# First weight piece loaded ahead of x, x transposed chunk by chunk as it lands, two M products issued earlier: a fused attention and MLP kernel on one Trainium2 core

## Chip, cores, metric

One core of a Trainium2 chip, everything in float32. The metric is device time in microseconds of one execution, median over runs. "Span" is the time from the first to the last instruction in the profile of one execution; it is about 1.8 us less than the time. Each run also records the mean clock granted to TensorE over its span: "full" is 1.00, "half" is 0.50, and a stretch at half clock is called a spell.

Engines: PE is TensorE's matmuls, PEld its weight loads, DVE VectorE, ACT ScalarE, POOL GpSimd, SP SyncE (here only a DMA queue).

## The reference, cut

```python
B, H, S, Ns, D = 8, 8, 512, 32, 64          # x: (B,H,S,D), state: (B,H,Ns,D)
scores  = x @ state.T / sqrt(D); a  = softmax(scores);  xread = a @ state
scores2 = state @ x.T / sqrt(D); a2 = softmax(scores2); sread = a2 @ x
t = concat([xread, sread], axis=2) as (B*(S+Ns), H*D) = 4352 tokens of 512
h = t @ w_in                                 # 512 x 2048, given as float64
g = h * sigmoid(1.702 * h)
out = g @ w_out                              # 2048 x 512, given as float64
```

The weights arrive as float64 words; DVE and ACT turn each piece of 128 rows and 512 columns into float32 ("rounding").

## The kernel before

The state of a batch is folded into w_in first: M = state x w_in (per chunk of 512 columns), then h = a x M, so that the token side needs two matmul steps per block and not four. Batches 0 and 1 run while the weights still come in; batches 2 to 7 then run on PE almost without holes. The parts that the change touches:

```python
def load_x(b):
    ...
    for c in range(SCH):                     # four chunks of 128 tokens
        queue = nc.scalar if b == 0 and c % 2 else nc.sync
        queue.dma_start(xn[b][:, c], x_v[b, c])

def round_a(i):                              # "power step" of piece i
    nc.vector.tensor_scalar(sc, hi, 0x7FF00000, None, ALU.bitwise_and)           # DVE
    ...                                      # w_in: two ACT instructions (Relu) finish it
def round_b(i):                              # the rest: four DVE instructions
    ...

def att_xT(b, j, warm=0):                    # transpose head pair j, all four chunks
    ps = att_ps([P, SCH, P], f"xT_{b}_{j}")
    for c in range(SCH):
        if warm: keep_warm(warm)             # filler matmuls, result unused
        nc.tensor.transpose(ps[:, c], x_heads(b, c, j), ident)
    (nc.vector.tensor_copy if b == 0 and j % 2 == 0 else nc.scalar.copy)(A[b]["xT"][:, j], ...)

def att_M(b, c, spare=False):                # 16 small matmuls, then two ACT copies
    ...
    for g in range(NG):
        nc.scalar.copy(m[:, g], ps[g])

def turn(b, c, then, n=()):                  # the four h products of batch b, chunk c
    for i in range(nper):
        if i == nper - 1 and then:
            att_M(*then)
        up_x(b, nper * c + i)
        if i < len(n): rounds(n[i])          # n[i] pieces rounded after product i

# ... opening
load_state(0); load_x(0); load_weights(NPR); load_state(1); load_x(1); load_weights(2 * NPR)
keep_warm(8)
att_state(0)
att_xT(0, 0, 2)
for j in range(1, NPR): att_xT(0, j)
att_scores(0)
powers_to(1); att_blocks(0); att_x_exp(0)    # softmax of batch 0 begins
powers_to(2); round_to(2, 1); att_x_norm(0)
keep_warm(24)
... # state, x and scores of batch 1
keep_warm(24)
powers_to(4); round_to(NPR, 2)               # pieces 0 to 3 rounded: chunk 0 complete
att_M(0, 0)
```

PSUM tiles of state, xT, M and eT share one pool of two buffers; h has two of its own. In the profiles, stT and xT are the transposed state and x, s the scores, aT the transposed softmax of the token side, e the exponentials (eT transposed), g the gelu of h, o the first products with w_out, and warm the filler. "later" and "sums" are buffers used for several things in turn.

## Time and profile before

| | before |
|---|---|
| time, median of the 4 runs beside the changed kernel | 803.94 us (802.64 to 805.23) |
| span of the profiled run, mean granted clock | 800.5 us, 0.997 |
| PE busy | 782.1 us (98%), of which part is filler |
| first h product starts | 34.99 us |
| first product with w_out ("o") starts | 88.67 us |

### The profile page before, as it was taken

The numbers are of one execution on the slowest core, as the hardware profiler recorded it, in microseconds if no ns is written. First come the engines' busy times: TensorE is split into PE (matmuls) and PEld (weight loads), VectorE is DVE, ScalarE is ACT, GpSimd is POOL, SyncE is SP. The second block draws the span as 40 slices with busy tenths as digits, with TensorE's granted clock in tenths as the row PEclk, the third lists the DMA queues.
The fourth block names the chain that finished last, engine by engine and source line by source line (L and its number), as shares of the span: only waits on it lengthen the run. The fifth ranks groups of instructions, "written<-read, shape, count | busy, mean of one in ns | idle before, by whom it ended". The sixth has DMA issues, their size and how long they took to land.

```text
span 800.5 us, 8798 instructions
## 1 busy us (share of the span) xinstructions
PE 782.1 (98%) x3618; PEld 530.4 (66%) x3620; DVE 314.4 (39%) x669; ACT 219.4 (27%) x394; POOL 36.1 (5%) x72
## 2 busy tenths in 40 slices
PE   8989999999999999999999999999999999999996
PEld 3333464467865878487856786487847788874785
DVE  3998899443404070226104340407022520312220
ACT  3676511023123141323133222314132312103100
POOL 0000000010100011000100011000100010010011
PEclk9999999999999999999999999999999999999998
DMA  9711345010030004000030003000300000010001
GB/s 238 293 54 52 105 137 133 1 52 1 27 83 0 1 17 91 1 1 14 27 69 1 1 28 83 0 1 14 84 9 1 14 27 14 0 23 5 1 14 39
DMA packets 43624, 35.17 MB, mean 44 GB/s; under 512 B 37312, under 2 KB 37312, under 8 KB 43584
## 3 DMA queue, kind: packets, MB, share of 16 engines
q1 hardware_dynamic: 37920, 25.17, 11.6%
q0 software_dynamic: 3584, 8.92, 3.4%
q10 hardware_dynamic: 2080, 0.52, 0.3%
q8 instruction: 28, 0.46, 0.2%
q14 instruction: 12, 0.10, 0.0%
HBM read 25.69 MB, written 8.91 MB: 43 GB/s over the span
## 4 chain that ended last, share of the span: by engine, by line
issue 69%; PE 22%; POOL 4%; DVE 2%; ACT 1%; DMA 1%; SPq 0%; POOLq 0%
PE h L404 7%; PE o L429 7%; POOL out_dram L491 4%; PE y L472 2%; PE x L472 2%; PE M L267 1%; PE z L472 1%; PE sr L359 1%; DMA xn<-in_x_dram 1%; PE xT L259 0%; ACT M L342 0%; PE s L267 0%; DVE w_in L199 0%; DVE w_in L198 0%; DVE later L197 0%
## 5 line engine op out<-in xcount | busy, mean ns | idle before, releaser
L404 PE MATMUL h<-aT,M 128*128 128x512 f32 x512 | 223.9, 594 | 5.8 <-ACT M L342 5.8
L404 PEld LDWEIGHTS h<-aT,M 128*128 128x128 f32 x512 | 96.5, 190 | 127.5 <-issue 113.6
L406 ACT ACTIVATE g<-h 128x512 f32<-128x512 f32 x120 | 71.5, 597 | 179.9 <-PE h L404 179.9
L472 PE MATMUL x<-w_out,g 128*128 128x256 f32 x448 | 100.0, 379 | 0.0
L472 PEld LDWEIGHTS x<-w_out,g 128*128 128x128 f32 x448 | 84.2, 190 | 13.9 <-issue 3.4
L453 DVE TENSOR_TENSOR later<-g,g 128x256 f32<-128x256 f32 (+1 forms) x64 | 26.1, 408 | 152.7 <-ACT g L406 152.7
L342 ACT COPY M<-M 128x512 f32<-128x512 f32 x64 | 33.2, 595 | 96.9 <-PE M L267 96.9
L491 POOL DMA_DIRECT2D out_dram<-osb x56 | 30.2, 543 | 541.7 <-ACT osb L488 359.7
L472 PE MATMUL z<-sums,later 128*128 128x256 f32 x224 | 51.1, 382 | 0.0
L472 PE MATMUL z<-w_out,g 128*128 128x256 f32 x224 | 50.8, 381 | 0.0
L472 PE MATMUL y<-sums,later 128*128 128x256 f32 x224 | 50.5, 379 | 0.0
L472 PE MATMUL y<-sums,g 128*128 128x256 f32 x224 | 50.5, 379 | 0.0
L472 PE MATMUL y<-w_out,g 128*128 128x256 f32 x224 | 50.1, 382 | 0.0
L472 PEld LDWEIGHTS y<-w_out,g 128*128 128x128 f32 x224 | 42.1, 190 | 10.5 <-issue 5.0
L472 PEld LDWEIGHTS z<-sums,later 128*128 128x128 f32 x224 | 42.1, 190 | 10.5 <-issue 5.0
L490 DVE TENSOR_TENSOR osb<-z,later 128x256 f32<-128x256 f32 x28 | 10.6, 420 | 92.3 <-PE z L472 92.3
L472 PEld LDWEIGHTS y<-sums,g 128*128 128x128 f32 x224 | 42.1, 190 | 5.5
L472 PEld LDWEIGHTS z<-w_out,g 128*128 128x128 f32 x224 | 41.6, 190 | 5.2
L472 PEld LDWEIGHTS y<-sums,later 128*128 128x128 f32 x224 | 41.6, 190 | 5.2
L499 DVE TENSOR_TENSOR later<-y,later 128x512 f32<-128x512 f32 x7 | 4.8, 692 | 87.8 <-PE y L472 87.8
L260 ACT COPY xT<-xT 128x512 f32<-128x512 f32 x30 | 17.6, 587 | 63.4 <-PE xT L259 63.4
L267 PE MATMUL M<-w_in,stT 64*32 64x512 f32 x512 | 33.7, 594 | 0.4 <-DVE w_in L199 0.4
(105 smaller groups left out, 748.6 us busy)
## 6 DMA issues: line engine op xcount, KB each, us to landing
later<-in_moe_w_out_dram SPq DMA_DIRECT2D x16, 512.0 KB
out_dram<-osb POOLq DMA_DIRECT2D x56, 128.0 KB, 2.0
xn<-in_x_dram SPq DMA_DIRECT2D x26, 256.0 KB
w_out<-in_moe_w_in_dram SPq DMA_DIRECT2D x12, 512.0 KB
later<-in_moe_w_in_dram SPq DMA_DIRECT2D x4, 512.0 KB
sums<-in_x_dram SPq DMA_DIRECT2D x4, 256.0 KB
out_dram<-osb POOLq DMA_DIRECT2D x4, 256.0 KB, 2.4
stn<-in_state_dram SPq DMA_DIRECT2D x16, 32.0 KB
```

Source lines behind the costliest of these rows:

```text
L260: (nc.vector.tensor_copy if b == 0 and j % 2 == 0 else nc.scalar.copy)(A[b]["xT"][:, j], ps.rearrange("p c q -> p (c q)"))
L267: nc.tensor.matmul(ps[g][st], A[b]["stT"][rows, st], rhs(rows, j), start=True, stop=True)
L342: nc.scalar.copy(m[:, g], ps[g])
L359: nc.tensor.matmul(ps[:, j], x_heads(b, c, j), a["eT"][:, :, c, Ns * j : Ns * (j + 1)], start=(c == 0), stop=(c == SCH - 1),)
L404: nc.tensor.matmul(hps, lhs[i], rhs[i], start=(i == 0), stop=(i == n - 1))
L406: nc.scalar.activation(out=gt[:, :ntok], in_=hps, func=AF.Gelu_apprx_sigmoid)
L429: nc.tensor.matmul(ops, G[key, f][:, P * r : P * (r + 1)], w_out[:, f], start=(f == 0), stop=(f == NF - 1))
L453: nc.vector.tensor_tensor(out=s1, in0=a21, in1=a22, op=ALU.add)
L472: nc.tensor.matmul(ps[:, r], lhs[f][:, P * r : P * (r + 1)], rhs[:, f], start=(first and r == 0 and f == 0), stop=(f == HF - 1), skip_grou ...
L490: nc.vector.tensor_tensor(out=o[:, r], in0=ps[:, r], in1=with_[:, r], op=ALU.add)
L491: nc.gpsimd.dma_start(dst(nb * i + r, slice(HN * k, HN * (k + 1))), o[:, r])
L499: nc.vector.tensor_tensor(out=k2, in0=Y, in1=k1, op=ALU.add)
```

## The change

Intent: give DVE its first piece of weights while it would otherwise wait for x; transpose x as it lands; and hide the copies of two M products behind an h product.

```diff
-            queue = nc.scalar if b == 0 and c % 2 else nc.sync
-            queue.dma_start(xn[b][:, c], x_v[b, c])
+            nc.sync.dma_start(xn[b][:, c], x_v[b, c])
...
+    def att_xT_arriving(b, warm):
+        A[b]["xT"] = apool.tile([P, NPR, S], FP32, tag="xT", name=f"xT_{b}")
+        for c in range(SCH):
+            keep_warm(warm)
+            ps = att_ps([P, NPR, P], f"xT_{b}_{c}")
+            for j in range(NPR):
+                nc.tensor.transpose(ps[:, j], x_heads(b, c, j), ident)
+            (nc.scalar.copy if c % 2 else nc.vector.tensor_copy)(A[b]["xT"][:, :, P * c : P * (c + 1)], ps)
...
+    load_weights(1)
     load_state(0)
     load_x(0)
...
-    keep_warm(8)
+    keep_warm(11)
+    round_to(1, 0)
     att_state(0)
-    att_xT(0, 0, 2)
-    for j in range(1, NPR):
-        att_xT(0, j)
+    att_xT_arriving(0, 2)
     att_scores(0)
-    powers_to(1)
+    powers_to(2)
...
-    turn(1, 1, None, [1])
     round_to(3 * NPR)
-    att_M(0, 2)
+    turn(1, 1, (0, 2), [1, 1])
+    round_to(4 * NPR)
     att_s_max(0)
     att_s_max(1)
-    turn(0, 2, None, [1, 1, 1])
-    round_to(4 * NPR)
-    att_M(0, 3)
+    turn(0, 2, (0, 3))
```

Cut: for batch 1 the fillers stand two ahead of each head pair now (before: three ahead of each transpose of the first pair); ahead of the second piece of the w_out stage, eT of a batch is issued before M.

More of the change, by code (lines that the diff above doesn't have):

```diff
@@ L250, in att_state, with att_xT @@
         nc.scalar.copy(A[b]["stT"], ps)
-    def att_xT(b, j, warm=0):
+    def att_xT(b, j):
         if j == 0:
@@ L256, in att_xT @@
         for c in range(SCH):
-            if warm:
-                keep_warm(warm)
             nc.tensor.transpose(ps[:, c], x_heads(b, c, j), ident)
-        (nc.vector.tensor_copy if b == 0 and j % 2 == 0 else nc.scalar.copy)(A[b]["xT"][:, j], ps.rearrange("p c q -> p (c q)"))
+        nc.scalar.copy(A[b]["xT"][:, j], ps.rearrange("p c q -> p (c q)"))
+    def att_xT_arriving(b, warm):
[6 more added lines that the diff above has]
+            (nc.scalar.copy if c % 2 else nc.vector.tensor_copy)(A[b]["xT"][:, :, P * c : P * (c + 1)], ps)
     def by_state(b, ps, rhs):
@@ L531 @@
     load_weights(2 * NPR)
-    keep_warm(8)
+    keep_warm(11)
+    round_to(1, 0)
     att_state(0)
-    att_xT(0, 0, 2)
-    for j in range(1, NPR):
-        att_xT(0, j)
+    att_xT_arriving(0, 2)
     att_scores(0)
-    powers_to(1)
+    powers_to(2)
     att_blocks(0)
     att_x_exp(0)
-    powers_to(2)
     round_to(2, 1)
@@ L545 @@
     att_state(1)
-    att_xT(1, 0, 3)
-    for j in range(1, NPR):
+    for j in range(NPR):
+        keep_warm(2)
         att_xT(1, j)
@@ L611 @@
             down(0, r, [f], out_x[0, r], r == SCH - 1)
-        if f in (0, nper * 2):
-            att_M(1, 2 + f // (nper * 2))
         if f in (0, 2):
@@ L616 @@
                 att_eT(f // 2, g)
+        if f in (0, nper * 2):
+            att_M(1, 2 + f // (nper * 2))
         if f in (1, 3):
```

## The prediction

> **What bounds the kernel now.** I read the page first, then the engines' busy time by windows, PE's waits, and the timelines of the first 90 us. The page says PE is busy 782.1 of 800.5 us, but its first 35 us include filler matmuls ("warm") that only keep the array awake. The windows separate the stages:
>
> ```profile
> 0.00:10.80 10.80, 8.08 (x23) 3.26 (x24) 0.28 (x2) 1.75 (x3) 0.77 (x8) 1.00 0.89 219
> 10.80:34.99 24.19, 22.30 (x136) 9.75 (x136) 21.96 (x36) 13.82 (x22) 0.00 (x0) 1.00 1.00 333
> 34.99:88.67 53.68, 48.55 (x177) 18.89 (x178) 47.33 (x96) 38.67 (x66) 0.00 (x0) 1.00 0.16 54
> 88.67:170.00 81.33, 80.60 (x276) 39.86 (x275) 62.43 (x126) 12.51 (x25) 1.52 (x3) 1.00 0.31 92
> 170.00:800.50 630.50, 622.61 (x3013) 458.66 (x3011) 182.43 (x412) 152.61 (x281) 33.80 (x62) 1.00 0.09 23
> ```
>
> Columns: window and length, busy us (and instructions) of PE, PEld, DVE, ACT, POOL, then clock, DMA share, GB/s. Until 10.80 DVE does nothing (0.28 us) and the DMA works; from 10.80 to 34.99 DVE is busy 21.96 of 24.19 us; from 34.99 PE does real work. After 88.67 PE has almost no holes, and the change leaves that code alone except one reordering. So 712 of the 800.5 us can only be moved as a block: what counts is when h starts, and the holes between 35 and 95. The timeline has the start:
>
> ```profile
> 12.58 1.79 PE L267 MATMUL s<-xT,stT 64*32 64x512 f32 x16
> ...
> 14.40 1.31 DVE L280 STREAM_TRANSPOSE e<-s 128x512 f32<-128x512 f32 x2 [1.10 <-PE s L267]
> ...
> 18.14 0.42 DVE L181 TENSOR_SCALAR later<-w_out 128x512 int32<-128x512 int32 x1
> ...
> 18.48 0.42 DVE L196 TENSOR_SCALAR w_in<-w_out 128x512 int32<-128x512 int32 x1
> 18.82 0.69 DVE L197 SCALAR_TENSOR_TENSOR later<-w_out,later 128x512 int32<-128x512 int32 x1
> ...
> 19.42 0.68 DVE L198 SCALAR_TENSOR_TENSOR w_in<-w_out,w_in 128x512 f32<-128x512 uint32 x1
> ...
> 20.14 0.69 DVE L199 SCALAR_TENSOR_TENSOR w_in<-w_in,later 128x512 f32<-128x512 f32 x1
> ...
> 32.52 0.69 DVE L199 SCALAR_TENSOR_TENSOR w_in<-w_in,later 128x512 f32<-128x512 f32 x1
> ...
> 33.27 1.05 PE L267 MATMUL M<-w_in,stT 64*32 64x512 f32 x4 [0.38 <-DVE w_in L199]
> ...
> 34.99 7.13 PE L404 MATMUL h<-aT,M 128*128 128x512 f32 x16 [0.67 <-ACT M L342]
> ```
>
> The start of each row is us from the span's start. The softmax of batch 0 cannot begin on DVE before the scores (14.40); from there DVE runs without a hole until the fourth w_in piece is rounded (32.52+0.69 = 33.21); then M, its copy, h. The path is x, scores, DVE, M. PE's later holes, from PE's waits and PE's own timeline:
>
> ```profile
> PE h L404 <- ACT M L342: 5.8, 5, 2.1
> PE eT L351 <- ACT M L342: 0.7, 1, 0.7
> ...
> 72.79 7.13 PE L404 MATMUL h<-aT,M 128*128 128x512 f32 x16 [0.75 <-ACT M L342]
> 79.85 1.09 PE L267 MATMUL M<-w_in,stT 64*32 64x512 f32 x16
> 81.69 7.13 PE L404 MATMUL h<-aT,M 128*128 128x512 f32 x16 [0.75 <-ACT M L342]
> ```
>
> Five times h waits for ACT's copy of M (us in total, times, longest): 0.67, 2.12, 1.50, 0.75, 0.75. The last two are M of chunks 2 and 3 of batch 0, which the change names.
>
> **What the Trainium skill says.** (1) "DMA: Bandwidth & Descriptors", section "Issuing engines are not separate DMA queues": queues of different engines share the same 16 DMA engines, so issuing from two saves only issue time. The trace agrees: x from two queues moved 217 to 278 GB/s between 3.5 and 7 us, x of batch 1 from one queue 246 GB/s (15 to 17). Putting all of x on one queue costs no bandwidth. (2) Same page, "Specifications": line rate wants 512 B or more per transfer. x comes in 256 B packets at 246 GB/s, w_in in larger ones at 410 to 418 GB/s (9 to 11): agrees, so the piece put ahead of x is cheap for its size. (3) "TensorE: Matmul & The Clock Gate", "Part 1": sustained activity ungates the clock. A warm matmul took 0.43 us before about 10 us and 0.21 us after (24 in 5.13). (4) Same page, "Architectural detail": ACT and DVE are strict FIFO. The trace agrees: at 76.80 DVE waited 3.06 us for an ACT result that was queued behind a gelu of a later product.
>
> **The change, part by part.**
>
> *Piece 0 of w_in ahead.* Its work on DVE (L196, L197, L198, L199) plus one power step (L181) runs now at 18.14 to 20.75, within the busy stretch: 2.6 us. Changed, piece 0 (512 KB, estimate 1.3 us at 410 GB/s) is first in the queue. First bytes moved at about 2.3 us, landings trail data by about 0.7 us (x's bytes were in at about 7.9, last chunk landed near 8.6), so I expect it at 4.7. DVE and ACT then round it at 4.8 to 8.8 while DVE was idle anyway. Another piece's power step takes the place of the one now at 12.85, so the stretch from the scores to M loses 2.6 us.
>
> *x by chunks.* The price: x's last chunk comes later, by 1.3 us less the about 0.5 us of w_in that already shared the engines: 8.6 + 0.8 = 9.4. Before, PE walked all four chunks head by head and four copies followed, so the last copy ended at 12.68+0.59 = 13.27 although x was there at 8.6. Now each chunk is transposed (4 matmuls) and copied (0.59 on ACT, 0.69 on DVE) on arrival; only the last chunk's copy follows its landing. Two PSUM buffers rotate: chunk 0's copy waits on DVE for piece 0's rounding (8.8), ends 9.5; chunk 2 transposes 9.5 to 10.0, chunk 3 after filler to 11.0, its copy to 11.7. All scores then need the last copy, so they no longer overlap copies: 1.1 us (16 such M matmuls take 1.09 when nothing interrupts), to 12.9. DVE's softmax starts at about 12.95 instead of 14.40: 1.4 us.
>
> Sum at M: 2.6 + 1.4 = 4.0; fourth piece ready at about 29.2, first h at 31.0. The filler count (11 instead of 8 at the head) is off this path, and later pieces keep their place in DMA order.
>
> *Does 4.0 us survive?* DVE runs without a hole from 14.40 to 73.7, so its whole stream moves with the start. M of chunk 1 needs piece 7 (rounded at 52.2 before, PE there at 53.1): both move together.
>
> *M of chunks 2 and 3 sooner.* Chunk 2's M goes before the last product of the previous chunk; it needs piece 11 (done 63.1) and PE would be there at 70.94-1.72 = 69.2 (old clock), so no new wait, and the copies (1.07) hide behind one product of 1.72 us. Saves 0.75. Chunk 3's M likewise, if piece 15 is there: today that is at 78.8, after four max reductions (3.15 us) and the 3.06 us wait; moving the reductions behind and issuing ACT's power steps earlier puts it at 63.1 + 0.34 + 4 x 2.27 = 72.5, PE needs it at 77. Saves 0.75. Together 1.5.
>
> *eT before M.* Today eT waits 0.73 us for M's copies in two shared PSUM buffers. Swapped, M waits for eT's copies instead: transposes 1.1, second copy ends about 0.7 after them. Zero gain.
>
> Sum: 4.0 + 1.5 = 5.5 us; I take 5.2 since the opening is a chain of small estimates.
>
> **Rivals.** *A, the early piece hurts:* rounding piece 0 holds DVE while chunk 0 waits for its copy, x lands late, and scores start no earlier than 12.6 with no overlap. For it: two PSUM buffers, strict order, and x's descriptors can hold up the issuing queue (one x issue of batch 1 took 3.36 us). Against it: x lands with over 2 us to spare today. Then only 2.6 + 1.5 less up to 1 remains: gain 3 to 4. *B, batch 1 becomes the next wait:* its x landed at 19.1 and PE now comes at about 18; taken head by head, the first group needs all four chunks. ACT's four copies then end near 23.2, and the next power step on ACT is wanted at 24.0. About 0.8 us spare; if missed, 0.5 to 1 us is lost. *C, DVE moves and PE does not:* if the new hole falls into ACT's copy queue, M's waits grow. ACT is busy 38.67 of 53.68 us there, so it has slack, and its order stays but for chunks 2 and 3: loss under 1 us. *D, all hidden, no change:* would need PE bound by its own work from 0; the 24 us of filler say no.
>
> **Range and chances.** Three runs before had 802.83, 805.05 and 805.23, the profiled one 802.3: spread 2.9 us, as large as half the effect. About 804 less 5.2 gives 798.8. With A and B together (gain 3) and the high mode 805.1: 802.1; with 6.5 and the low mode: 795.8. A gain over 2% needs 16 us, all of the holes and most of the filler stretch; a loss of 16 us would need a second DMA stall; neither is in sight: 0.01 each.
>
> **What would show it.** Right: DVE's piece-0 rows before 9 us, softmax start near 13.0, fourth piece near 29.2, first h near 31.0; waits of h for M's copy down from 5 to 3 and from 5.8 to about 4.3 us; no DVE wait of 3 us near 75; eT's 0.7 wait now on M; after the first o all shifted by about 5.5. Wrong: softmax start at 14 or later (A), a DVE hole between 18 and 29 (B), new PE waits at chunk 2 or 3 (C). The prediction fails most easily on the size of the opening step, or if runs sit in another mode of the 2.5 us spread.

## The result

| | before | changed |
|---|---|---|
| time, median of 4 runs | 803.94 us (802.64 to 805.23) | 797.01 us (796.72 to 798.55) |
| span of the profiled run, clock | 800.5 us, 0.997 | 795.2 us, 0.998 |
| softmax of batch 0 starts (DVE) | 14.40 | 12.70 |
| fourth piece rounded | 33.21 | 28.90 |
| first h | 34.99 | 31.35 |
| first o | 88.67 | 83.38 |

The ratio is 0.9918, 95% interval 0.9893 to 0.9942. A ratio is the mean time of one kernel's runs over that of the other's of the same rounds, so it is not quite the ratio of the medians. This is a gain of about 0.8%: 6.6 us of 803.94. It is small, but the interval leaves out 1.

The windows of the changed kernel by stage (window and length, busy us and instructions of PE, PEld, DVE, ACT, POOL, clock, DMA share, GB/s):

```profile
0.00:12.70 12.70, 10.45 (x53) 4.45 (x54) 4.57 (x11) 4.25 (x7) 0.77 (x8) 1.00 0.89 226
12.70:31.35 18.65, 17.07 (x103) 7.74 (x104) 18.30 (x29) 11.20 (x18) 0.00 (x0) 1.00 1.05 330
31.35:83.38 52.03, 48.41 (x177) 18.89 (x177) 46.21 (x94) 38.21 (x65) 0.00 (x0) 1.00 0.23 82
```

DVE now works 4.57 us before the softmax (2.03 before the change), and the stage from the first h to the first o took 52.03 instead of 53.68 us. From the first o to the end it is 795.2 - 83.38 = 711.8 us against 800.5 - 88.67 = 711.8: the block moved unchanged. DVE's timeline (start, busy us, engine, line, operation, [idle before, and what ended it]):

```profile
5.34 0.43 DVE L180 TENSOR_SCALAR later<-w_out 128x512 int32<-128x512 int32 x1 [4.20 <-DMA w_out<-in_moe_w_in_dram]
...
12.70 1.31 DVE L287 STREAM_TRANSPOSE e<-s 128x512 f32<-128x512 f32 x2
...
28.21 0.69 DVE L198 SCALAR_TENSOR_TENSOR w_in<-w_in,later 128x512 f32<-128x512 f32 x1
```

Piece 0 arrived at 5.34 and was rounded before the softmax. From the softmax start to the fourth piece it is 28.90 - 12.70 = 16.20 us, before 33.21 - 14.40 = 18.81: the 2.6 us are out. PE's timeline:

```profile
29.51 1.09 PE L274 MATMUL M<-w_in,stT 64*32 64x512 f32 x16
31.35 7.13 PE L411 MATMUL h<-aT,M 128*128 128x512 f32 x16 [0.76 <-ACT M L349]
...
65.59 1.09 PE L274 MATMUL M<-w_in,stT 64*32 64x512 f32 x16
66.61 7.13 PE L411 MATMUL h<-aT,M 128*128 128x512 f32 x16
73.67 1.09 PE L274 MATMUL M<-w_in,stT 64*32 64x512 f32 x16
74.69 8.85 PE L411 MATMUL h<-aT,M 128*128 128x512 f32 x20
```

The h that follow M at 65.59 and 73.67 carry no wait. M of chunk 0 starts at 29.51, though its last piece was ready at 28.90. PE's waits (us in total, times, longest):

```profile
PE h L411 <- ACT M L349: 4.4, 3, 2.1
```

So two traces differ by 5.3 us, and the runs by 6.6 us. Both differences need an account.

### The profile page after: what moved, and what is told of

It is laid out like the page before. It is cut to its first block, busy times and chain, and to the rows that moved or that the text cites. A ratio compares the mean times of both kernels' runs of the same rounds, so it can differ in the third digit from the quotient of the medians. Undisturbed runs are those within 1.5% of the kernel's fastest.

```text
span 795.2 us, 8800 instructions
## 1 busy us (share of the span) xinstructions
PE 779.6 (98%) x3617; PEld 529.8 (67%) x3619; DVE 314.4 (40%) x669; ACT 219.3 (28%) x394; POOL 35.9 (5%) x72
## 4 chain that ended last, share of the span: by engine, by line
issue 69%; PE 22%; POOL 4%; SPq 2%; ACT 1%; DMA 1%; POOLq 0%; DVE 0%
PE h L411 7%; PE o L436 7%; POOL out_dram L498 4%; PE y L479 2%; PE x L479 2%; PE M L274 1%; SPq L129 1%; PE z L479 1%; PE sr L366 1%; PE warm L113 1%; DMA sums<-in_x_dram 1%; PE xT L256 0%; PE s L274 0%; SPq L158 0%; SPq L121 0%
```

## The experiments

All kernels gave correct results. Each was timed beside the kernel before on its chip; the first four share one chip, the rest another. "h to o" is the time from the first h to the first o.

### Batch 1: taking the change apart

**m_only**: the kernel before, with only the later part.

```diff
-    turn(1, 1, None, [1])
     round_to(3 * NPR)
-    att_M(0, 2)
+    turn(1, 1, (0, 2), [1, 1])
+    ...                          # as in the change, eT ahead of M too
```

> The kernel before with only the later part of the change (M of chunks 2 and 3 of batch 0 one product sooner, max reductions behind the rounding, eT ahead of M). Theory 1 (the two parts are independent and add): first h stays at 34.99, the two waits of 0.75 us for M's copies and the DVE wait of 3.06 us near 76.8 are gone, the first o starts at about 87.0 instead of 88.67, span about 798.9 (1.6 less). Rival (the later part works only because the opening brought DVE forward): piece 15 is not ready when PE comes for it, M of chunk 3 gets a wait on DVE, and the span falls by less than 0.8 us.

Measured: 803.32 us (801.16 to 803.74), ratio 0.9984 (0.9964 to 1.0005), profiled span 801.8: by the times alone no gain is shown, since the interval holds 1. The waits are as expected (h waits three times, 4.3 us; no DVE wait near 75), but the first h started at 36.23 and h to o took 53.72 us. The windows of this run show why:

```profile
44.20:47.61 3.41, 1.29 (x16) 0.33 (x6) 3.38 (x6) 3.35 (x6) 0.00 (x0) 1.00 0.00 0
47.61:51.02 3.41, 3.41 (x5) 1.35 (x4) 3.31 (x7) 0.35 (x2) 0.00 (x0) 0.50 0.01 2
```

In the second window the granted clock is 0.50. That group of h products took 8.83 instead of 7.13 us, a loss of 1.70; without it h to o is 52.02, exactly the changed kernel's 52.03. Full clock at the start was recorded from 13.49 us, in the profile of before from 10.09; the opening code is the same, yet the softmax of batch 0 began at 15.63 instead of 14.40, and the first h 1.24 later. So the expected span failed, but not the part: the later part is worth 53.68 - 52.02 = 1.66 us without the changed opening, and the rival (piece 15 not ready) is out: no wait of M on DVE appears there.

**opening_only**: the changed kernel with the later part put back (the inverse of the edit above, on the changed kernel).

> The changed kernel with the later part put back as before. Theory 1 (independent parts): softmax of batch 0 starts on DVE at 12.7, first h at 31.35, both waits of 0.75 us are there again, the first o starts at about 85.0, span about 796.9 (3.6 less than before). Rival (the opening's gain is given back later, because ACT's queue or DVE and not PE sets the pace from 35 to 88): first o later than 86 and a span above 798.

Measured: 799.95 us (798.88 to 800.65), ratio 0.9951 (0.9934 to 0.9968), span 797.1. First h 31.58, both waits of 0.75 us back, first o 85.26: h to o is 53.68, as before. The rival (gain given back later) is out. The parts are independent: opening 3.4 us here (3.6 in the changed kernel), later part 1.65. One expectation missed: the softmax started at 13.29, not 12.7. The change puts the power step of the second piece ahead of it in DVE's order (`powers_to(2)`), and here DVE waited 2.27 us for that piece, until 12.95. In the changed kernel it waited for it too, until 12.35. So how early the softmax starts also hangs on the landing of that piece.

**no_piece_ahead**: the changed kernel, first piece after x again.

```diff
-    load_weights(1)
     load_state(0)
...
-    round_to(1, 0)
...
-    powers_to(2)
+    powers_to(1)
     att_blocks(0)
     att_x_exp(0)
+    powers_to(2)
     round_to(2, 1)
```

> The changed kernel with the first piece of w_in loaded and rounded after x again; x is still taken by chunks on one queue. Theory 1 (2.6 us of DVE work leave the busy stretch, and x comes about 1.3 us later for it): last chunk of x used at about 9 instead of 10.2, softmax starts at about 11.3, but the stretch from there to the fourth piece is 18.8 instead of 16.2 us, fourth piece at about 30.1 instead of 28.9; first h at 31.9 to 32.5 instead of 31.35; span 0.5 to 1.2 above the changed kernel's 795.2. Rival (the piece ahead is the whole opening gain, the chunks nothing): first h at 34 or later, span 798 or more. Rival 2 (filler matmuls and not DVE hold M in the changed kernel): first h within 0.3 of 31.35.

Measured: 799.48 us (797.91 to 800.00), ratio 0.9944 (0.9927 to 0.9961), span 798.2. Softmax at 12.06 (0.6 earlier than with the piece ahead, where 1.4 was expected), fourth piece at 30.89, stretch 18.83, first h 32.66. So the piece ahead is worth 32.66 - 31.35 = 1.3 us net: 2.6 won in the stretch, 0.6 paid for the later x, and 0.7 that a later wait swallows (see fill_18). The profiled run again has 3.4 us at half clock, from 44.61; its fastest run, at clock 0.998, has a span of 796.1, 0.9 over the changed kernel's, in the expected range. Both rivals are out: the first h came neither at 34 or later nor within 0.3 of 31.35. Without the piece ahead, the rest of the opening still brings the softmax from 14.40 to 12.06.

**by_heads**: the changed kernel, batch 0 transposed by head pairs again.

```diff
-    att_xT_arriving(0, 2)
+    for j in range(NPR):
+        keep_warm(2)
+        att_xT(0, j)             # copies on DVE and ACT in turn, as before
```

> The changed kernel with x of batch 0 transposed head pair by head pair again, all chunks needed by the first group; the piece of w_in is still ahead. Theory 1: last chunk lands at about 10, four groups and four copies follow it, softmax starts at 13.3 to 13.6 instead of 12.70, fourth piece at about 29.6; since filler holds M until 29.5 anyway, first h moves by 0.1 to 0.9, span 795.3 to 796.1. Rival (copying each chunk on arrival is what the opening gains): softmax at 14.4 or later, first h at 33 or later, span 797 or more.

Measured: 802.49 us (800.14 to 802.71), ratio 0.9975 (0.9956 to 0.9994), span 800.9 at clock 0.991. This missed by far: softmax at 17.44, first h at 35.42. The window shows it:

```profile
8.73:15.56 6.83, 5.95 (x20) 3.79 (x20) 2.42 (x5) 0.59 (x1) 0.00 (x0) 0.50 1.01 303
```

PE waits for x four times (2.6 us in all), loses the clock that it had from 5.32, and runs the transposes of batch 0 at half clock until 15.56. Two of six runs had clock 0.996 and a span of 798.4, still some 3.2 over the changed kernel. All three signs of the rival came (softmax, first h, span). But this run is not the old order: the kernel before had two fillers ahead of each of the first four transposes, where x arrives, and this one has none between them. What it shows is that PE needs work while x is still coming, transposes or filler, or it can lose the clock. How much of the 4.1 us in the first h is missing filler, how much is clock and how much is order this run does not separate. The old order with its filler, in the changed kernel, was not run; nor were the changed fillers of batch 1 alone.

### Batch 2: clock, filler, and ACT's queue

**after_again**: the changed kernel, unchanged.

> The changed kernel once more, as the yardstick of this batch. Theory 2 (the spread of 2 us between runs is the clock: a spell of 3.4 us at half clock near 40 to 50 us, where PE has its longest hole of 2.1 us, and an early or late ungating at the start): spans of 795.0 to 795.5 at mean clock 0.998, and of about 796.8 at 0.994 to 0.996 in the runs that catch the spell; the kernel before, in the same rounds, has most runs at 0.995 and about 1.7 us more than its clean 799.4 to 800.5. Rival (the spread is memory or launch noise): the same spans occur without any relation to the clock.

Measured: 796.51 us (796.24 to 797.04), ratio 0.9918 (0.9900 to 0.9935). All five runs at clock 0.998, spans 794.5 to 795.2. The kernel before on this chip: of 11 runs two at 0.997 (spans 799.2 and 800.7), six at 0.995 with 800.8 to 801.0, three at 0.995 with 803.0 to 803.5. The clock does divide the runs, as theory 2 said, but not alone: the two groups at 0.995 differ by a further 2.4 us. The record of the clock begins only when it is first full, so a late start of the full clock does not show in the mean; traces with 8 fillers at the head have it at 9.75, 10.1 and 13.5, those with 11 at 4.1 to 7.1, and I take that to be the second difference. For untraced runs this is inference. One caution in reading the mean: every trace ends with 2.5 to 5.7 us at half clock, after the last matmul, which alone makes the mean 0.998 to 0.996. A spell of 3.41 us takes off another 0.002. With ends of that length, 0.994 or 0.995 means a spell, but 0.996 can be either (m_only's trace has one, relus_moved's below has none).

**head_8**: the changed kernel with 8 fillers at the head.

```diff
-    keep_warm(11)
+    keep_warm(8)
```

> The changed kernel with 8 instead of 11 filler matmuls at the head. Theory 2b (the three more fillers bring the ungating of the clock forward to 6.6 us from 10.1 or 13.5): full clock is recorded from about 10 or later in most runs, transposes and scores of batch 0 take up to twice as long, softmax starts 0.4 to 2 us later than 12.70, span 795.6 to 797.5. Rival (fillers at the head are off the path, as the prediction took them): clock from 6.6 as before, softmax within 0.2 of 12.70, span within 0.3 of the changed kernel's.

Measured: 798.72 us (797.24 to 798.96), ratio 0.9938 (0.9919 to 0.9956). Full clock recorded from 9.75, softmax at 13.47; yet the first h at 31.44, only 0.1 later: in the changed kernel the filler behind the scores of batch 1 holds M for 0.6 us anyway, and that takes up most of the 0.77. The cost came elsewhere: 3.41 us at half clock from 43.88. Two of six runs, at 0.998, have a span of 795.5. So the three fillers matter, not through the path that they lie on but through when full clock is granted.

**When the half-clock spell strikes.** The one at PE's longest hole is always 3.41 us near 44 to 51 us. Counting steps of that length (3.413 us over the ten steps of m_only) from the moment at which full clock is first recorded, each trace has one step that holds most of PE's hole of 2.12 us (the wait of h for M of batch 1, chunk 0):

| kernel | part of the hole in one step, us | PE busy in that step, us | next step at half clock |
|---|---|---|---|
| before | 1.80 | 1.61 | no |
| opening_only | 1.70 | 1.71 | no |
| changed | 1.68 | 1.74 | no |
| changed, again | 1.38 | 2.04 | no |
| fill_18 | 1.25 | 2.16 | no |
| by_heads | 1.96 | 1.46 | yes |
| head_8 | 1.99 | 1.42 | yes |
| m_only, no_piece_ahead, two_queues | 2.12 | 1.29 | yes |

Ten traces of ten: with 1.80 us or less of the hole in one step the clock stays, with 1.96 or more it halves. This holds for this hole and is no general threshold: in by_heads the step from 5.32, while x arrives, had PE busy for 1.64 us, and the next step was at half clock. The change did not remove this hole. It moved the hole and the steps. That the hole falls across a boundary in nearly all runs of the changed kernel is seen in two traces and inferred for the others from their clock.

**fill_18**: the changed kernel with 18 fillers after the scores of batch 1 instead of 24.

> The changed kernel with 18 instead of 24 filler matmuls after the scores of batch 1. Theory 3 (filler issued late, because x of batch 1 came late, holds M until 29.5 though the fourth piece is ready at 28.9): fillers end near 28.2, three quarters of M are done before 28.9, M ends near 30.0, first h at 30.6 to 30.8 instead of 31.35, span 0.6 less. Rival (M waits for DVE or ACT anyway): first h within 0.2 of 31.35.

Measured: 797.92 us (796.23 to 798.61), ratio 0.9929 (0.9912 to 0.9947), profiled span 794.5. PE's timeline:

```profile
28.04 1.95 PE L274 MATMUL M<-w_in,stT 64*32 64x512 f32 x16
30.66 7.13 PE L411 MATMUL h<-aT,M 128*128 128x512 f32 x16 [0.67 <-ACT M L349]
```

M starts before the last piece is ready, and h at 30.66, 0.7 earlier. So filler did hold M, by 0.6 us: batch 1's x came late (PE waited 0.7 us for it), the scores of batch 1 ended late, and 24 fillers stood behind them in PE's order. But the median got worse: four of six runs are at 0.994 to 0.996, with spans of 796.1 to 796.8. Won on the path, lost on the clock (the trace is of a run without a spell; that the four had one is inferred from clock and span).

**relus_moved**: power steps moved in ACT's queue. ACT's timeline in the changed kernel says why:

```profile
39.02 0.71 ACT L185 ACTIVATE later<-later,edge 128x512 f32<-128x512 int32 x1
39.76 0.72 ACT L186 ACTIVATE later<-later,edge 128x512 int32<-128x512 f32 x1
40.39 0.71 ACT L185 ACTIVATE later<-later,edge 128x512 f32<-128x512 int32 x1
41.13 0.72 ACT L186 ACTIVATE later<-later,edge 128x512 int32<-128x512 f32 x1
41.76 1.05 ACT L349 COPY M<-M 128x512 f32<-128x512 f32 x2
```

M of batch 1 was done on PE at 40.25, but its copies stand behind two pairs of power steps and start at 41.76.

```diff
     att_x_exp(1)
+    powers_to(7)
     up_x(0, 0)
...
-    round_to(2 * NPR)
+    round_to(2 * NPR, 2)
     att_M(0, 1)
```

> The changed kernel with ACT's power steps of one piece put ahead of the first gelus, and those of another behind M of chunk 1, so that M's copies wait for less on ACT. Theory 4 (the holes of 2.12 and 1.50 us in front of h are ACT's queue, two and one pairs of power steps of 1.4 us each ahead of the copies): holes of 0.8 to 1.0 and 0.75; first o at about 81.3 instead of 83.4, span about 793.2; and with the long hole gone no run has a half-clock spell near 40 to 50 us (clock 0.998 in all). Rival (DVE is the next bound): a wait of M of chunk 1 on DVE's rounding takes up over half of the gain, span 794.3 or more.

Measured: 795.89 us (795.82 to 796.01), ratio 0.9909 (0.9890 to 0.9928), span 794.1. Both holes shrank as expected, to 0.75 and 0.76, and all four spans lie within 0.1 of each other. But only part of the gain came: the first h was at 30.94 and h to o took 51.28, 0.75 less instead of 2. PE's timeline has the rest, a new hole:

```profile
59.08 5.42 PE L411 MATMUL h<-aT,M 128*128 128x512 f32 x12 [1.22 <-ACT M L349]
```

The second pair of power steps now stood before another copy of M. PE did not wait for DVE, so the stated rival is out, and theory 4 had not looked one copy further.

### Batch 3: the version that beats both, and what is left

**relus_moved_2**: as relus_moved, and one more piece's power steps moved behind a copy.

```diff
-    turn(0, 1, (1, 1), [1, 1, 1])
+    turn(0, 1, (1, 1), [1, 1])
```

> As relus_moved, and one more pair of ACT's power steps (piece 13) moved from before to behind M of chunk 1 for batch 1, where relus_moved showed a new hole of 1.22 us. Theory 4 (the holes in front of h are the power steps that stand before M's copies in ACT's queue, and moving one onto another copy only moves the hole): that hole shrinks to 0.3 or less, those of 0.75 stay, first o at about 81.2 instead of 82.2, span about 793.0, all runs within 0.3. Rival (ACT as a whole is out of slack there): the hole turns up again elsewhere, span 793.7 or more.

Measured: 795.25 us (794.90 to 795.47), ratio 0.9901 (0.9884 to 0.9918), span 793.4. The hole of 1.22 is gone; one of 0.50 came at 61.86, where h waits for a gelu that stands behind the moved steps. First o at 81.56 where 81.2 was expected. Both are half right: moving work off one copy helps, and ACT's slack there is nearly used up. The six spans run from 793.1 to 793.7, twice the scatter expected.

**best**: relus_moved_2 with 18 instead of 24 fillers.

> relus_moved_2 with 18 instead of 24 fillers after the scores of batch 1. Theory 3 and 4 together: first h at 30.66, span 792.6 to 792.9; and since the hole of 2.12 us is gone, no run has the half-clock spell that four of six runs of fill_18 seem to have had, so all runs lie within 0.4. Rival (fewer fillers themselves bring on the half clock): runs split in two groups 1.5 us or more apart, as in fill_18.

Measured: 794.99 us (794.83 to 795.02), ratio 0.9897 (0.9878 to 0.9917), spans 793.1 to 793.2, clock 0.997 to 0.998. First h at 30.64. No run split off: fewer fillers alone do not bring the half clock. h waits for M's copies 2.1 us in all (4.4 in the changed kernel) and 0.5 for a gelu.

Against relus_moved_2 the gain of 0.2 is not clear; the span is under the changed kernel's 794.5 to 795.2 by 1.3 us or more in every run, and the median time by 1.5.

**best_no_fill**: best without these fillers.

```diff
     att_scores(1)
-    keep_warm(18)
```

> best without any fillers after the scores of batch 1: PE is idle for 4.7 us ahead of M. Theory 2c (the filler is what keeps the clock up): half clock is recorded from about 27 to 34, M and the first products of h take twice as long (about 0.85 instead of 0.43 us each), first o 1.5 to 3.4 us later than in best. Rival (filler has no use here): first h at 30.66, first o as in best, clock 0.998.

Measured: 797.96 us (795.04 to 798.08), ratio 0.9926 (0.9904 to 0.9949), span 796.3, clock 0.992.

```profile
29.57:36.39 6.82, 6.16 (x10) 2.19 (x7) 6.72 (x11) 4.61 (x6) 0.00 (x0) 0.50 0.87 351
```

Two steps at half clock, the first h group takes 9.68 instead of 7.13 us, the first o comes 3.1 us later than in best. Filler without a result is worth 3 us here. One run of four escaped, with a span of 793.3. PE's small matmuls of 32 columns filled 1.49 us of the step from 22.74 and the clock stayed; they filled 1.53 of the next and it fell. So busy time in the profile is no exact measure of what the clock follows.

**two_queues**: the changed kernel, chunks 1 and 3 of x on ACT's queue as before.

```diff
-            nc.sync.dma_start(xn[b][:, c], x_v[b, c])
+            queue = nc.scalar if b == 0 and c % 2 else nc.sync
+            queue.dma_start(xn[b][:, c], x_v[b, c])
```

> The changed kernel with chunks 1 and 3 of x on ACT's queue again, as in the kernel before; piece 0 is still first on the other queue. Theory 1b (queues share the same engines, so one queue costs nothing): x is complete within 0.5 us of the same time, but piece 0 shares the engines with x from the start and lands about 1 us later (6.3 instead of 5.3), its rounding ends at about 9.8 and softmax starts within 0.7 us of 12.70; span within 0.8 of the changed kernel's. Rival (the second queue gives bandwidth or issue time): softmax starts 0.7 us or more earlier than 12.70.

Measured: 800.31 us (800.04 to 801.99), ratio 0.9968 (0.9948 to 0.9989), span 800.2. Both theories missed: neither a gain nor a tie, but a loss of most of the opening. First h at 34.66; two runs at clock 0.998 still have spans of 798.5 and 798.6. PE's waits:

```profile
PE stT L248 <- DMA stn<-in_state_dram: 3.1, 1, 3.1
```

Piece 0 landed as before (DVE at 5.47), but the small state, behind piece 0 on one queue, did not get through beside x on the other; PE sat idle for 3.1 us, and the record has half clock from 8.89 to 12.30. The DMA queues of this kernel from 5 to 6 us (q1 is SP's, q10 ACT's; packets, MB, share of 16 engines):

```profile
q10 hardware_dynamic: 989, 0.25, 116.7%
q1 hardware_dynamic: 106, 0.03, 12.6%
```

So the one queue is not a neutral part of the change: with a piece of weights in front, it keeps state and x in order.

## Why the prediction was right

The measured median, 797.01, lies inside 795.8 to 802.1, 1.8 under the 798.8 named. By its steps:

- **Piece 0 ahead.** Predicted to land at 4.7 and be rounded by 8.8; it was there at 5.34 and rounded at 9.46. The stretch lost 2.61 us, predicted 2.6. Right.
- **x by chunks.** Softmax predicted at 12.95, measured 12.70: a gain of 1.70 instead of 1.4. The time was right, the reason only in part, and that is luck. With 8 fillers at the head (head_8, one trace) the softmax started at 13.47, so 0.93 of the 1.70 came without the three new fillers and 0.77 with them, through the clock; the prediction had called them "off this path". It also took the late copies before the change for order alone, where half clock until 10.09 had a part.
- **Sum at M.** Fourth piece predicted at 29.2, measured 28.90. First h predicted at 31.0, measured 31.35. The term that was mis-sized is the step from the fourth piece to h, 1.78 us before and 2.45 after: the 24 fillers between the scores of batch 1 and M, which the prediction's sum leaves out, held M by 0.6 us. fill_18 recovered it.
- **M sooner.** Predicted 1.5, measured 1.65 by h to o, and 1.66 in m_only once the spell is taken off. The waits of h went from 5 to 3 and from 5.8 to 4.4 us (predicted 4.3); piece 15 was ready at 68.33 and used at 73.67.
- **eT before M.** Predicted to move a wait of 0.7 and gain nothing. M waited 0.24; first o to second o went from 6.32 to 6.21 us. A tenth, so nearly right.
- **Rivals.** A (late softmax) did not happen. B did in small: PE waited 0.7 us for x of batch 1, DVE did not, and the wait cost time only through the filler behind it. C did not happen. D's "24 us of filler" is the length of the stretch from 10.80 to 34.99; filler keeps PE busy for 13.3 us of it, and for 20.7 from the start. The argument stands with these.
- **One queue costs nothing.** Right as far as it went, and too weak: two_queues lost most of the opening.
- **The sum.** 5.2 predicted, 5.3 between the two profiles. The runs differ by 6.6. The further 1.3 is what the prediction called the spread of 2.9 us and left as noise. The profile of before was a clean one at 0.997. In the 23 further runs of before on two chips, three are at 0.997 and 20 at 0.994 or 0.995; of nine runs of the changed kernel eight are at 0.998. At 1.70 us a spell, estimated from m_only, 20/23 against 1/9 makes 1.48 against 0.19, a difference of 1.3. But the four runs of before that stand in the result have no clock on record. That the other runs had the same spell as the traced ones is inferred from their clock, and the effect of a late first full clock is not in this sum; so the agreement is closer than the argument.

Left open: what exactly the clock counts as activity, and why chips and launches differ in when full clock is first granted.

## What to carry to other kernels

Read the start of the block that cannot shrink and the holes in front of it; work moved into an engine's idle opening leaves the busy stretch in full (2.6 us here), but its transfer can delay others (0.6) and a wait further on, filler included, can swallow some (0.7). Before you trust a difference of one or two us, look at the granted clock of every run and at where PE's longest hole lies: a change can gain or lose a half-clock spell without touching its cause. When a queue is in strict order, follow moved work to the next thing that stands behind it, for the hole moves there.

## What the Trainium skill lacked or had wrong

- "TensorE: Matmul & The Clock Gate", section "Why this matters for your kernels", advises against PE-idle gaps of over about 3 us. Here a hole of 2.12 us was enough, in five traces where 1.96 to 2.12 us of it fell in one step of 3.41 us (PE busy 1.29 to 1.46 us of it, in part with matmuls of 32 columns); with 1.80 us or less of this hole in one step it never was. The length of the spells, 3.41 and 6.83 us, agrees with the window length of the same page's Part 1.
- "DMA: Bandwidth & Descriptors", section "Queues, rings and completion order", says that an engine takes turns between the queue rows that have work. In two_queues ACT's row moved 989 packets between 5 and 6 us and SP's 106, while the state waited on SP's row until PE could use it at 8.96. Whether SP's descriptors were there to be taken is not shown by any run, so this may be the issuing side and not the turns; the page does not tell a reader to expect it. The advice of the same page's section "Issuing engines are not separate DMA queues", that a second queue saves only issue time, leaves out that it can also cost: 3.1 us of PE's wait here.
